# Sliding-window attention with soft expert mixing: logits a period later and ahead of the scores, the flip of x between two parts of the values, slot steps behind the second maxima

## The chip, the core and the metric

One core of a Trainium2 chip runs the whole program in one launch. The metric is the device time of that launch in microseconds (us); smaller is better. The time before is the median of three executions: 292.3 us (291.13 to 292.62).

## The reference

```python
scores = (q @ k.T) / 8                        # per batch and head, 8 x 8 of 576 x 64
scores = where(0 <= i - j < 128, scores - slope[head] * |i - j|, -1e9)
attn   = exp(scores - rowmax) / (rowsum + 1e-9)
x      = (attn @ v) as (8*576 tokens, 512)
logits = x @ phi                              # 512 x 32: 8 experts of 4 slots
d      = softmax of logits over all 4608 tokens
slot_input = d.T @ x                          # 32 x 512
slot_out[e] = relu(slot_input[e] @ w1[e]) @ w2[e]     # w1: 512 x 1024, w2: 1024 x 512
out    = (softmax of logits over the 32 slots) @ slot_out
```

Each query sees itself and the 127 keys before it. The softmax over all tokens needs every logit, so the expert layers can only begin once the attention of all tiles is done; the sums for the slots are kept as running maxima and running sums meanwhile.

## The kernel before

The program has two parts: a loop over 36 attention tiles, and a tail in which the weights w1 and w2 meet the 32 slot inputs and the output is written. A tile is 128 query rows (64 queries of each of two groups) with all 8 heads. Tile number t of a batch (t = 0 to 4) says which keys it sees; tile t = 0 sees no keys before its own, so its score products are narrower and its values have no second part.

Five engines work in their own order, which the order of the Python calls sets by hand (a manual schedule; nothing reorders the calls of one engine). The loop `for k in range(n)` (L589 to L632) is a software pipeline; one turn is called a period here. In period k the engines do, for different tiles:

- TensorE: `flip` (L299, products at L303) transposes the exponentials of tile k-1, group 0 into PSUM bank a, group 1 into bank b. `x_flip` (L361, products at L365) transposes the finished attention rows of tile k-3 into bank a again, so it has to wait until the copy of group 0 has left that bank. `values` (L325) multiplies by v for tile k-2, into banks e and o, in two parts: 32 products against whole blocks (L335; the PE queue records each of the 16 listed products in two passes), then 32 against half blocks (L345), which close the sums. Tile t = 0 has only the first part. Then `scores` for tile k+1, group 0 and group 1: the slope ramp (L233) and q times k (L246). They overwrite the score banks that the exponentials of tile k have read.
- ScalarE: `take` copies both groups of transposed exponentials out of PSUM (L306), `expo` computes the exponentials of tile k (L284, four per group), `x_keep` copies the transposed x (L368).
- GpSimd: `split` masks the copies in eight half-tile steps (L319, L322) and clears one column of a weight tile (L146), which gates the weight's load.
- VectorE: `chain` for each group of tile k, which is `merge` (L260), `rowmax` (L267) and `bias` (L272); then `x_store` of tile k-2 (L356 to L359), which divides by the row sums and frees banks e and o.
- SyncE issues all loads: q two tiles ahead, k a batch ahead, v four tiles ahead, and 35 of the weight units spread over the periods.

Every fourth tile closes a group q of four tiles for the expert part. Its steps are put into the periods by `do(when, k, ...)` (L567 to L580) and run by `run(when, k)` at named places of the loop: `logits` (L370, products at L375, into bank b) after the scores of period 4q+6, `token_copy` on ScalarE (L381) and `token_max` on VectorE (L386 to L390) after it, `token_exp` on ScalarE (L397); a period later `token_flips` (L416) and `slot_sum` (L428), both in bank b, `token_keep` (L422), `slot_add` (L438), and then the slot softmax on VectorE in small steps (`slots_max`, L450 and L451; `slots_norm`, L460 to L463), which are put into a list of fillers. At most four fillers were run at the end of each period, which is ahead of the next period's `chain`.

The buffers that matter: finished x rows have six places (`xns`, tile number modulo 6), transposed x four (`xts`, tile number modulo 4), and the PSUM banks a, b, e and o have one buffer each.

Of the kernel before, what the change touches and what calls it, by code (L numbers as in the profile page):

```python
# [25 lines left out]
NPAIR = H // 2  # L26
# [6 lines left out]
NQ = NTT // 4  # L33
# [32 lines left out]
def tile_attn_softmoe(  # L66
# [82 lines left out]
    st = {}  # L149
    last = B - 1  # L150

    def order(b):
        return (1, 2, 3, 4, 0) if b == last else range(4 + b % 2)

    tiles = [(b, t) for b in range(B) for t in order(b)]
# [103 lines left out]
    def merge(k, g, us=ALL):  # L259
        nc.vector.copy_predicated(  # L260
            window(k, g, us, 0, KB), bc(mask_le, 1, len(range(4)[us])), window(k, g, us, P, KB))
# [28 lines left out]
    def filler():  # L290
        if fillers:
            fillers.pop(0)()

    def chain(k, g):
        merge(k, g)
        rowmax(k, g)
        bias(k, g)
# [27 lines left out]
    def values(k, to=None):  # L325
        b, t = tiles[k]
        x = st["x", k] = to or [bank(tag, [P, NPAIR, VD], "xp") for tag in ("e", "o")]
        for j in range(NPAIR):
            for par in range(2):
                for g in range(2):  # L330
                    if t == 4:
                        v = (v3_even, v_slot[b, 3])[g]
                    else:
                        v = v_slot[b, t - 1 + g if t else 0]
                    nc.tensor.matmul(  # L335
                        x[par][half[g], j], lhsT=pas[k % 2][:, g, par, j], rhs=v[:, par, j],
                        start=(j == 0), stop=(t == 0 and j == NPAIR - 1))
        if t == 0:
            return
        for j in range(NPAIR):  # L340
            for par in range(2):
                for g in range(2):
                    rows = half[corner(k, g, par)]
                    v = (v4_even, v4_odd)[g] if t == 4 else v_slot[b, t - g]
                    nc.tensor.matmul(  # L345
                        x[par][half[g], j], lhsT=pps[k % 2][rows, g, j], rhs=v[rows, par, j],
                        start=False, stop=(j == NPAIR - 1))
# [121 lines left out]
    def drain():  # L469
        while fillers:  # L470
            filler()
# [57 lines left out]
    def do(when, k, fn, *a):  # L529
        todo.setdefault((when, k), []).append((fn, a))  # L530

    def run(when, k):
        for fn, a in todo.pop((when, k), []):
            fn(*a)
# [30 lines left out]
            load_v_tails(b + 1)  # L565

    for q in range(NQ - 1):  # L567
        k = 4 * q + 3
        do("post", k + 3, logits, q)
        do("act", k + 3, token_copy, q)  # L570
        do("dve", k + 3, token_max, q)
        do("late", k + 3, token_exp, q)
        do("dve", k + 4, token_sum, q)
        do("turn2", k + 4, token_flips, q)
        do("keep", k + 4, token_keep, q)
        do("mid", k + 4, slot_sum, q, "b")
        do("dve", k + 4, slot_add, q)
        do("dve", k + 4, later, slots_max, q)
        do("act", k + 5, slots_exp, q)
        do("dve", k + 5, later, slots_norm, q)  # L580
    for k in range(n - 3):
        do("turn", k + 3, x_flip, k)
        do("x_keep", k + 3, x_keep, k)
# [1 line left out]
    with tc.manual_schedule(engines=ORDERED):  # L585
# [3 lines left out]
        for k in range(n):  # L589
            if k:  # L590
                chain(k, 0)
            else:
                for us in (LO, HI):
                    merge(k, 0, us)
                    rowmax(k, 0, us)
                    bias(k, 0, us)
                    expo(k, 0, us)
            chain(k, 1)
            if k:
                flip(k - 1, 0, "a")  # L600
                flip(k - 1, 1, "b")
                run("turn", k)
                run("turn2", k)
            if k:
                take(k - 1, 0, nc.scalar.copy)
                split(k - 1, 0)
                load_weights_at(k, 1)
                take(k - 1, 1, nc.scalar.copy)
                split(k - 1, 1)
                load_weights_at(k, 2)  # L610
                expo(k, 0)
            run("keep", k)
            expo(k, 1)
            run("x_keep", k)
            if k >= 2:
                values(k - 2)
                after_values(k - 2)
            run("mid", k)
            if k + 1 < n:
                scores(k + 1, 0)  # L620
                scores(k + 1, 1)
                loads(k + 1)
            if k == n - 2:
                load_weight()
            run("post", k)
            if k >= 2:
                x_store(k - 2)
            run("act", k)
            run("dve", k)
            run("late", k)  # L630
            for _ in range(4):
                filler()  # L632

        ka, kb, kc = n - 3, n - 2, n - 1
        lp = free[3]
# [15 lines left out]
        x_flip(ka)  # L651
        x_keep(ka)
        values(kb)
        for _ in range(5):
            load_weight()
        values(kc, [x.rearrange("p (j d) -> p j d", d=P)[:, :, 0:VD] for x in (free[0], free[2])])
        x_store(kb)
        run("act", n)
        run("dve", n)
        x_store(kc, (0,))  # L660
# [277 lines left out]
```

## Time and profile before

| | |
|---|---|
| median of 3 executions | 292.3 us |
| the profiled execution's own time | 293.59 us |
| span of its records, first to last instruction | 291.9 us |
| time outside the span (293.59 - 291.9) | 1.69 us |
| TensorE matmuls busy | 253.2 us (87%) |
| VectorE busy | 178.9 us (61%) |
| ScalarE busy | 158.2 us (54%) |
| GpSimd busy | 97.6 us (33%) |
| mean granted TensorE clock | 0.994 |

The attention loop fills the span to about 222 us, the rest is the tail. In timelines a row gives start, time, engine, line, operation, operands and count, and in square brackets how long the engine stood idle before it and what ended that. PE is TensorE's products, PEld its weight loads, DVE VectorE, ACT ScalarE, POOL GpSimd. A weight load runs ahead of its product, so TensorE's pace from group to group is read from the starts of the PEld rows.

### The profile page before, as it was taken

What the parts mean: (1) busy time and instruction counts of PE and PEld (TensorE: products, weight loads), DVE (VectorE), ACT (ScalarE), POOL (GpSimd) and SP (SyncE); (2) the same over time, 40 slices, a digit from 0 to 9 for tenths busy, and PEclk for the clock granted to TensorE, in tenths of its full rate; (3) what the DMA queues carried; (4) which work ended last, traced back from release to release, by engine and by line L of the source; (5) the groups of instructions that cost most, each with busy time, mean ns of one, the idle gap of its engine ahead of it and who ended that gap; (6) DMA issues with size and microseconds to landing.
All of it is one profiled execution on the core that took longest, in us unless ns stands there. A gap on an engine that the chain in (4) does not pass through costs nothing.

```text
span 291.9 us, 12240 instructions
## 1 busy us (share of the span) xinstructions
PE 253.2 (87%) x5088; PEld 183.5 (63%) x5088; DVE 178.9 (61%) x550; ACT 158.2 (54%) x481; POOL 97.6 (33%) x269
## 2 busy tenths in 40 slices
PE   7688898988989897898899989989979889999980
PEld 3466776776777586666667757767766532566640
DVE  3566566775794875589478577657865741224461
ACT  2567756666755776656667566866565201013350
POOL 0046344541660566045417541645544001000000
PEclk9999999999999999999999999999999999999997
DMA  6769975788688477668776858855755999998895
GB/s 177 233 223 273 387 255 170 257 248 269 197 288 285 143 252 236 213 199 268 266 246 189 277 178 260 261 186 154 246 168 183 307 395 305 409 372 308 342 384 234
DMA packets 30715, 74.74 MB, mean 256 GB/s; under 512 B 3650, under 2 KB 5698, under 8 KB 30660
## 3 DMA queue, kind: packets, MB, share of 16 engines
q1 hardware_dynamic: 29940, 73.48, 75.5%
q8 instruction: 40, 0.66, 0.9%
q10 hardware_dynamic: 720, 0.48, 0.6%
q14 instruction: 15, 0.12, 0.1%
HBM read 64.51 MB, written 9.44 MB: 253 GB/s over the span
## 4 chain that ended last, share of the span: by engine, by line
PE 64%; DVE 14%; ACT 14%; issue 4%; DMA 1%; ACTq 0%; DVEq 0%
PE s L246 11%; PE xp L335 10%; PE xq L365 6%; ACT area L306 6%; PE op L772 5%; PE xp L345 5%; ACT area L284 5%; PE hp L736 5%; PE pt L303 5%; PE s L233 4%; PE po L793 4%; DVE nb L267 3%; PE lp L375 3%; PE ap L428 3%; DVE s L260 2%
## 5 line engine op out<-in xcount | busy, mean ns | idle before, releaser
L284 ACT ACTIVATE area<-s,nb 128x128 f32<-128x128 f32 x288 | 81.3, 393 | 9.5 <-DVE nb L272 8.2
L322 POOL TENSOR_SCALAR_AFFINE_SELECT area<-area 64x256 f32<-64x256 f32 x112 | 46.4, 414 | 116.1 <-ACT area L306 110.5
L306 ACT COPY area<-pt 128x512 f32<-128x512 f32 x71 | 38.0, 585 | 46.8 <-PE pt L303 46.0
L246 PE MATMUL s<-kq 64*64 64x192 f32 (+2 forms) x1088 | 53.7, 314 | 0.8 <-DMA kq<-k_t 0.8
L267 DVE TENSOR_REDUCE nb<-s 128x4 f32<-128x512 f32 (+1 forms) x73 | 49.9, 684 | 2.6
L319 POOL TENSOR_SCALAR_AFFINE_SELECT area<-area 64x256 f32<-64x256 f32 x112 | 46.1, 412 | 7.5
L246 PEld LDWEIGHTS s<-kq 64*64 64x64 f32 x1088 | 40.2, 138 | 3.8 <-DMA kq<-k_t 1.4
L335 PE MATMUL xp<-va,area 128*64 128x66 f32 x1120 | 40.9, 225 | 1.1 <-issue 1.1
L335 PEld LDWEIGHTS xp<-va,area 128*64 128x64 f32 x1120 | 35.7, 137 | 7.2 <-issue 4.0
L303 PE MATMUL pt<-unit_r,area 128*128 128x128 f32 x288 | 39.7, 280 | 0.6 <-DVE acc L438 0.6
L365 PE MATMUL xq<-unit_r,xs 128*128 128x128 f32 x144 | 23.7, 286 | 18.1 <-ACT area L306 17.0
L303 PEld LDWEIGHTS pt<-unit_r,area 128*128 128x128 f32 x288 | 30.7, 141 | 10.8 <-issue 7.9
L260 DVE COPY_PREDICATED s<-cst,s 128x256 f32<-128x256 int32 (+1 forms) x73 | 30.7, 420 | 9.1 <-PE s L246 8.9
L356 DVE TENSOR_SCALAR rs<-xp 128x4 f32<-128x4 f32 x70 | 8.7, 161 | 39.8 <-PE xp L345 36.4
L233 PE MATMUL s<-ramp 64*64 64x384 bf16 x288 | 26.5, 342 | 6.5 <-ACT area L284 5.6
L365 PEld LDWEIGHTS xq<-unit_r,xs 128*128 128x128 f32 x144 | 15.3, 141 | 26.2 <-ACT area L306 24.8
L359 DVE TENSOR_TENSOR xs<-xp,rs 128x256 f32<-128x256 f32 x70 | 26.5, 420 | 1.2
L368 ACT COPY xs<-xq 128x512 f32<-128x512 f32 (+1 forms) x36 | 22.7, 631 | 1.1 <-PE xq L365 1.0
L233 PEld LDWEIGHTS <-ramp 64*64 64x64 bf16 x288 | 11.6, 107 | 17.3 <-issue 15.8
L799 DVE COPY ob<-po 128x384 f32<-128x384 f32 x24 | 12.3, 553 | 13.1 <-PE po L793 12.5
L345 PE MATMUL xp<-va,area 64*64 64x66 f32 x896 | 19.6, 224 | 0.0
L799 ACT COPY ob<-po 128x384 f32<-128x384 f32 x24 | 10.3, 482 | 13.6 <-PE po L793 13.6
(112 smaller groups left out, 254.5 us busy)
## 6 DMA issues: line engine op xcount, KB each, us to landing
w<-w SPq DMA_DIRECT2D x49, 512.0 KB, 5.5
va<-v_n SPq DMA_DIRECT2D x36, 264.0 KB, 4.8
out<-ob SPq DMA_DIRECT2D x24, 384.0 KB, 4.1
kq<-q_t SPq DMA_DIRECT2D x35, 256.0 KB, 3.8
kq<-k_t SPq DMA_DIRECT2D x32, 256.0 KB, 4.3
xs<-w SPq DMA_DIRECT2D x5, 512.0 KB, 6.5
area<-w SPq DMA_DIRECT2D x4, 512.0 KB, 8.2
kt<-k_t SPq DMA_DIRECT2D x4, 384.0 KB, 5.2
```

Of the source, the lines that this page charges most:

```text
L233: nc.tensor.matmul(parts[par][half[c], :, 0:WIN], lhsT=slope[rows, c], rhs=steps[rows, 0 if t else 1 + g], start=True, stop=False)
L246: nc.tensor.matmul(parts[par][half[c], jh, KB * o:WIN], lhsT=qt[rows, j], rhs=keys, start=False, stop=(jh == 1))
L260: nc.vector.copy_predicated(window(k, g, us, 0, KB), bc(mask_le, 1, len(range(4)[us])), window(k, g, us, P, KB))
L267: nc.vector.tensor_reduce(s["nb"][:, 4 + us.start:4 + us.stop], window(k, g, us, 0, P), axis=AX.X, op=ALU.max, negate=True)
L284: nc.scalar.activation(dst, window(k, g, u, 0, P).rearrange("p (a w) -> p a w", a=2), AF.Exp, bias=s["nb"][:, u:u + 1], scale=SCALE)
L303: nc.tensor.transpose(s["pt"][:, u], s["p4"][:, u], ident)
L306: copy(pas[k % 2][:, g].rearrange("p a j m -> p (a j m)"), st[k, g]["pt"].rearrange("p u w -> p (u w)"))
L319: nc.gpsimd.affine_select(dst, pa, [[0, NPAIR], [-1, KB]], ALU.is_gt, 0.0, base=0, channel_multiplier=1)
L322: nc.gpsimd.affine_select(dst, pa, [[0, NPAIR], [1, KB]], ALU.is_ge, 0.0, base=0, channel_multiplier=-1)
L335: nc.tensor.matmul(x[par][half[g], j], lhsT=pas[k % 2][:, g, par, j], rhs=v[:, par, j], start=(j == 0), stop=(t == 0 and j == NPAIR - 1))
L345: nc.tensor.matmul(x[par][half[g], j], lhsT=pps[k % 2][rows, g, j], rhs=v[rows, par, j], start=False, stop=(j == NPAIR - 1))
L365: nc.tensor.transpose(st["xq", k][:, P * j:P * j + P], xns[k % NXN][:, P * j:P * j + P], ident)
```

## The change

The second part of the values becomes a function of its own (`values_ex`, L339, products at L347), and the calls of a period are put in another order. Numbers of the lines behind it rise by 2 in the functions (`x_flip` at L367, logits at L377, slot sums at L430).

```diff
-        if t == 0:
-            return
-        for j in range(NPAIR):
+
+    def values_ex(k):
+        b, t = tiles[k]
+        x = st["x", k]
+        for j in range(NPAIR if t else 0):
...
     for q in range(NQ - 1):
-        k = 4 * q + 3
-        do("post", k + 3, logits, q)
-        do("act", k + 3, token_copy, q)
-        do("dve", k + 3, token_max, q)
-        do("late", k + 3, token_exp, q)
-        do("dve", k + 4, token_sum, q)
-        do("turn2", k + 4, token_flips, q)
-        do("keep", k + 4, token_keep, q)
-        do("mid", k + 4, slot_sum, q, "b")
-        do("dve", k + 4, slot_add, q)
-        do("dve", k + 4, later, slots_max, q)
-        do("act", k + 5, slots_exp, q)
-        do("dve", k + 5, later, slots_norm, q)
+        k = 4 * q + 6 + (q < NQ - 2)
+        do("mid" if q < NQ - 2 else "post", k, logits, q)
+        do("act", k, token_copy, q)
+        do("dve", k, token_max, q)
+        do("late", k, token_exp, q)
+        do("dve", k + 1, token_sum, q)
+        do("turn2", k + 1, token_flips, q)
+        do("keep", k + 1, token_keep, q)
+        do("mid", k + 1, slot_sum, q, "b")
+        do("dve", k + 1, slot_add, q)
+        do("dve", k + 1, later, slots_max, q)
+        do("act", k + 2, slots_exp, q)
+        do("dve", k + 2, later, slots_norm, q)
...
             chain(k, 1)
+            for _ in range(4):
+                filler()
             if k:
                 flip(k - 1, 0, "a")
                 flip(k - 1, 1, "b")
-                run("turn", k)
-                run("turn2", k)
+            if k >= 2:
+                values(k - 2)
+            run("turn", k)
+            run("turn2", k)
...
             expo(k, 1)
-            run("x_keep", k)
             if k >= 2:
-                values(k - 2)
+                values_ex(k - 2)
                 after_values(k - 2)
             run("mid", k)
+            run("x_keep", k)
...
             run("late", k)
-            for _ in range(4):
-                filler()
...
         values(kb)
+        values_ex(kb)
...
         x_store(kb)
+        drain()
         run("act", n)
```

On TensorE the order inside every period changes. This is a period of the second batch, around one `x_flip`; xp is written by the values, xq by `x_flip`, s by the scores, pt by `flip`:

```order
 L246 MATMUL s_1_87<-kq 64x128 x8
 L303 MATMUL pt<-unit_r,area 128x128 x8
-L365 MATMUL xq<-unit_r,xs 128x128 x4
-L335 MATMUL xp<-va,area 64x66 x16
-L345 MATMUL xp<-va,area 64x66 x16
+L335 MATMUL xp<-va,area 64x66 x16
+L367 MATMUL xq<-unit_r,xs 128x128 x4
+L347 MATMUL xp<-va,area 64x66 x16
 L233 LDWEIGHTS ramp
 L233 MATMUL s_0_86<-ramp 64x2x192
```

The first part of the values now stands between the transposes of the exponentials and those of x, and the second part behind the latter.

On TensorE around the logits of the first group (lp), before: they stand behind the scores, and the next period has the flips of the logits (dp) and the slot sums (ap).

```order
L246 MATMUL s_1_87<-kq 64x192 x8
L375 MATMUL lp<-xs,phi 32x128 x16
L303 MATMUL pt<-unit_r,area 128x128 x8
L365 MATMUL xq<-unit_r,xs 128x128 x4
L416 MATMUL dp<-unit_r,lg 128x128 x2
L335 MATMUL xp<-va,area 64x66 x16
L345 MATMUL xp<-va,area 64x66 x16
L428 MATMUL ap<-xs,dn 32x512 x4
```

The same logits in the changed kernel, one period later:

```order
L303 MATMUL pt<-unit_r,area 128x128 x8
L335 MATMUL xp<-va,area 64x66 x16
L367 MATMUL xq<-unit_r,xs 128x128 x4
L347 MATMUL xp<-va,area 64x66 x16
L377 MATMUL lp<-xs,phi 32x128 x16
L233 LDWEIGHTS ramp
L233 MATMUL s_0_86<-ramp 64x2x192
```

They now stand ahead of that period's scores. For the last group but one (q = 7) they stay in period 34 behind the scores.

On VectorE, behind the first slot steps, before: the four steps of `slots_norm` (cs, ln) stand between `x_store` (xs) and the next maxima (nb).

```order
L359 TENSOR_TENSOR xs<-xp,rs 128x256 x2
L460 TENSOR_REDUCE cs<-ln 128x4
L461 TENSOR_SCALAR cs<-cs 128x4
L462 RECIPROCAL cs<-cs 128x4
L463 TENSOR_TENSOR ln<-ln,cs 128x128
L260 COPY_PREDICATED s_0_86<-cst,s_0_86 128x4x64
L267 TENSOR_REDUCE nb<-s_0_86 128x4
```

The same steps in the changed kernel:

```order
L260 COPY_PREDICATED s_1_87<-cst,s_1_87 128x4x64
L267 TENSOR_REDUCE nb<-s_1_87 128x4
L272 TENSOR_SCALAR nb<-nb 128x4
L462 TENSOR_REDUCE cs<-ln 128x4
L463 TENSOR_SCALAR cs<-cs 128x4
L464 RECIPROCAL cs<-cs 128x4
L465 TENSOR_TENSOR ln<-ln,cs 128x128
L358 TENSOR_SCALAR rs<-xp 128x4 x2
```

They stand behind both groups' maxima and ahead of the next `x_store`. The order of ScalarE and of GpSimd inside a period stays; the group steps alone come one period later there. Because the slot sums of group q are now read in period 4q+8, and `x_store` of that same period writes tile 4q+6 into the place of tile 4q, that `x_store` has to wait for the slot sums.

## The prediction

> **What bounds the kernel now.** I read the page first, then the waits summed by pair, then the rows of single periods.
>
> ```profile
> PE 253.2 (87%) x5088; PEld 183.5 (63%) x5088; DVE 178.9 (61%) x550; ACT 158.2 (54%) x481; POOL 97.6 (33%) x269
> ```
>
> Of the span of 291.9 us TensorE works 87% and the next engine 61%, so what TensorE waits for in the loop is what can be won. The summed waits name it (total us, times, longest):
>
> ```profile
> PEld xq L365 <- ACT area L306: 24.8, 33, 1.5
> ...
> ACT lg L381 <- PE lp L375: 16.3, 8, 3.4
> ...
> ACT area L284 <- DVE nb L272: 8.2, 12, 3.2
> ...
> PE s L233 <- ACT area L284: 5.6, 10, 1.8
> ```
>
> The flip of x waits in every period for ScalarE's copy out of bank a, 24.8 us in all. The two next rows delay ScalarE: it stands for the logits, and for late maxima. The last is TensorE waiting to overwrite scores that are still being read. Now one period without group steps on TensorE, by its weight loads:
>
> ```profile
> 199.68 0.86 PEld L303 LDWEIGHTS pt<-unit_r,area 128*128 128x128 f32 x8 [0.28 <-issue]
> 201.06 0.42 PEld L365 LDWEIGHTS xq<-unit_r,xs 128*128 128x128 f32 x4 [0.53 <-ACT area L306]
> 201.65 1.01 PEld L335 LDWEIGHTS xp<-va,area 128*64 128x64 f32 x32 [0.17 <-POOL area L322]
> 202.73 0.56 PEld L345 LDWEIGHTS xp<-va,area 64*64 64x64 f32 x32
> 203.20 0.12 PEld L233 LDWEIGHTS <-ramp 64*64 64x64 bf16 x4
> 203.26 0.64 PEld L246 LDWEIGHTS s<-kq 64*64 64x64 f32 x16
> 203.91 0.13 PEld L233 LDWEIGHTS <-ramp 64*64 64x64 bf16 x4
> 204.07 0.64 PEld L246 LDWEIGHTS s<-kq 64*64 64x64 f32 x16
> 204.99 0.31 PEld L303 LDWEIGHTS pt<-unit_r,area 128*128 128x128 f32 x3 [0.28 <-issue]
> ```
>
> The next flips start at 204.99, so the period is 204.99 - 199.68 = 5.31 us. Of that 0.53 us is the wait for the copy; the work is 4.78 us. The same stretch on ScalarE, VectorE and GpSimd:
>
> ```profile
> 200.43 1.07 ACT L306 COPY area<-pt 128x512 f32<-128x512 f32 x2 [2.80 <-PE pt L303]
> 201.39 2.19 ACT L284 ACTIVATE area<-s,nb 128x128 f32<-128x128 f32 x8
> ```
> ```profile
> 203.47 0.25 DVE L356 TENSOR_SCALAR rs<-xp 128x4 f32<-128x4 f32 x2 [1.31 <-PE xp L345]
> 203.75 0.20 DVE L357 RECIPROCAL rs<-rs 128x8 f32<-128x8 f32 x1
> 203.99 0.76 DVE L359 TENSOR_TENSOR xs<-xp,rs 128x256 f32<-128x256 f32 x2
> 204.66 0.28 DVE L460 TENSOR_REDUCE cs<-ln 128x4 f32<-128x128 f32 x1
> ...
> 205.60 0.42 DVE L260 COPY_PREDICATED s<-cst,s 128x256 f32<-128x256 int32 x1
> ```
> ```profile
> 204.61 0.41 POOL L322 TENSOR_SCALAR_AFFINE_SELECT area<-area 64x256 f32<-64x256 f32 x1
> ```
>
> VectorE does the slot steps from 204.66 to 205.60, 0.94 us, while the next scores already wait for their maxima. In periods where this is later still, the exponentials are late, and TensorE with them.
>
> **The first part of the values ahead of the flip of x.** Counted from the start T of a period's flips: the first copy starts at T + 0.75 (200.43) and lets the flip of x go at T + 1.38 (201.06). In the new order 0.86 us of flips, a gap of 0.17 and 1.08 us of values come first, so the flip of x can start at T + 2.11, when the copy is 0.7 us old. The 24.8 us go. What is ready for the values? Their copies and masks are a period old: GpSimd's last mask ends at 204.61 + 0.41 = 205.02, T + 5.34, and the next values start at the next T + 0.86, which is T + 5.86 if a period is 5.0: 0.5 us to spare. Banks e and o are freed at 203.99 + 0.76 = 204.75, T + 5.1: 0.8 us to spare. Lateness beyond that would be paid in full in each period. SyncE's issues keep their places; the loads of v wait for the second part as before.
>
> The order costs changes of operand shape. Now there are flips to x flips, x flips to values (0.17 gap), and values part to part (0.07). After: flips to values, values to x flips, x flips to second part. Gaps at changes lie between none and 0.28 us in the rows above, so the extra is between 0 and 2 x 0.28 - 0.17 = 0.39; I take 0.2, one gap like that ahead of L335. TensorE's period becomes 4.78 + 0.2 = 4.98.
>
> **What is late next: ScalarE.** The exponentials end at 201.39 + 2.19 = 203.58, T + 3.90, and scores of group 1 may not start before. How a period looks that is held by that:
>
> ```profile
> 59.35 2.40 ACT L284 ACTIVATE area<-s,nb 128x128 f32<-128x128 f32 x8 [1.07 <-DVE nb L272]
> 61.79 0.36 PE L233 MATMUL s<-ramp 64*64 64x384 bf16 x4 [0.25 <-ACT area L284]
> 62.73 0.86 PEld L303 LDWEIGHTS pt<-unit_r,area 128*128 128x128 f32 x8 [0.28 <-issue]
> ```
>
> The scores go 0.04 us after the exponentials, and the next flips 0.94 us later. So ScalarE allows a period of 3.90 + 0.04 + 0.94 = 4.88. That this ring turns at such a pace is seen at the start, in a period with no x to flip:
>
> ```profile
> 16.82 1.09 PE L303 MATMUL pt<-unit_r,area 128*128 128x128 f32 x8
> ```
> ```profile
> 21.71 1.09 PE L303 MATMUL pt<-unit_r,area 128*128 128x128 f32 x8
> ```
>
> 21.71 - 16.82 = 4.89 us. The two limits, 4.98 and 4.88, lie close; a quiet period is 5.0 us. Without second part it is held at 4.89; with narrow scores it gains a third of the 0.64 us load of group 1 and is 4.67 (an estimate from 128 columns in place of 192).
>
> **Slot steps behind the second maxima.** This takes up to 0.94 us from the path of `x_store` to the maxima. VectorE then does the steps while it would wait for the values (1.31 us idle before 203.47), so they cost nothing; without that idle time 0.94 us once in four periods, 7 us in all. The maxima of group 1 have to be there at T + 2.8, when ScalarE has done half of its 2.19 us.
>
> **Logits ahead of the scores, a period later.** One group's rows:
>
> ```profile
> 190.96 0.81 PEld L375 LDWEIGHTS lp<-xs,phi 128*32 128x32 f32 x32 [0.28 <-issue]
> 191.97 0.88 PEld L303 LDWEIGHTS pt<-unit_r,area 128*128 128x128 f32 x8 [0.20 <-issue]
> 192.11 0.27 ACT L381 COPY lg<-lp 128x128 f32<-128x128 f32 x1 [2.08 <-PE lp L375]
> ```
> ```profile
> 194.37 0.42 PEld L365 LDWEIGHTS xq<-unit_r,xs 128*128 128x128 f32 x4 [1.52 <-ACT area L306]
> ```
> ```profile
> 195.71 0.40 ACT L422 COPY dn<-dp 128x256 f32<-128x256 f32 x1
> ```
> ```profile
> 197.93 0.11 PEld L233 LDWEIGHTS <-ramp 64*64 64x64 bf16 x4 [0.84 <-issue]
> ```
>
> The copy of the logits came only with the next flips, ScalarE stood 2.08 us for it, its copies of the flips were late, and TensorE stood 1.52 us. In the new order the logits are done one pair of scores (1.79 us, 203.20 to 204.99) earlier, under ScalarE's own `x_keep`; the copy, maximum and exponential then end just as the next flips are ready. That `x_keep` now waits for the logits, whose place it overwrites; they end about 0.4 us after the exponentials, off the path. The logits themselves stay 1.01 us of TensorE, plus 0.1 for changed gaps: 6.1 us for such a period. The period behind it lasted from 191.97 to 199.68, 7.71 us; less 1.52 it is 6.19, plus 0.2 for the shapes and 0.1 because the slot sums now come so early that they wait for the 0.40 us copy of the flipped logits: 6.5. A new wait is that of `x_store` for the slot sums in that period. Behind it on VectorE stand the running sums and the next maxima; the sums end about 1.0 us after the values do, and the maxima of group 0 are needed at the next T + 1.7 (201.39), so I take zero (bounds 0 and 1.0 us, seven times).
>
> **The sum.** Flips in the rows of the loop:
>
> ```profile
> 26.33 1.09 PE L303 MATMUL pt<-unit_r,area 128*128 128x128 f32 x8
> ```
> ```profile
> 210.50 1.09 PE L303 MATMUL pt<-unit_r,area 128*128 128x128 f32 x8
> ```
> ```profile
> 222.15 0.66 PE L303 MATMUL pt<-unit_r,area 128*128 128x128 f32 x4
> ```
>
> From period 4 to the end of period 35 the loop takes 222.15 - 26.33 = 195.8 us. After: 16 quiet periods (11 at 5.0, 2 at 4.89, 3 at 4.67) 78.8; 7 with logits (5 at 6.1, 2 without second part, 0.47 and a gap of 0.15 less, at 5.48) 41.5; 7 with slot sums (3 at 6.5, 2 narrow, two thirds of group 0's 0.64 and a third of group 1's less, at 5.86, 2 without second part, held by the copy, at 6.35) 43.9; the last two, where the logits stay behind the scores, 11.6 as before (222.15 - 210.50). Together 175.8, a gain of 20.0 us. I take two things off. TensorE also stood without a wait that the trace names:
>
> ```profile
> 29.44 1.04 PE L335 MATMUL xp<-va,area 128*64 128x66 f32 x28 [0.80 <-issue]
> ```
> ```profile
> 114.04 0.33 PE L365 MATMUL xq<-unit_r,xs 128*128 128x128 f32 x1 [1.11 <-issue]
> ```
> ```profile
> 21.70:38.50 16.80, 14.91 (x352) 12.34 (x348) 10.76 (x33) 11.09 (x33) 7.30 (x21) 1.00 0.98 325
> 38.50:222.20 183.70, 163.64 (x3589) 127.68 (x3585) 130.16 (x409) 120.65 (x376) 85.17 (x230) 1.00 0.72 226
> ```
>
> These stalls, 1.9 us, I leave in. And up to 38.5 us the DMA engines are busy 0.98 of the time (last but one column) with 325 GB/s: there the loads cannot come 2 us earlier. I take 1.0 off (bounds 0 and 2.2). In the rest of the loop the share is 0.72 and would be about 0.80. The tail keeps its work; its two slot steps now stand ahead of the last `x_store` (0.6 us late), while the last slot sums come up to 0.7 earlier: zero.
>
> 20.0 - 1.9 - 1.0 = 17.1 us. The profiled execution, 293.59 us (span 291.9 and 1.69 outside), would be 276.5; it lay 1.3 above the median, so the median would be 292.3 - 17.1 = 275.2, called 275.
>
> **The rivals.**
> *The wait moves to the maxima.* VectorE is busy 130.16 us of 183.70 in the loop, 71%, and would be 79% of 165. If `x_store` and the maxima slip, the exponentials wait again, as in the 8.2 us row. A loss of 0.25 us in 28 periods is 7 us: 282. For it: that row; against it: 1.31 us of idle time before `x_store`.
> *Shape changes cost a whole product.* The upper bound of 0.39, plus as much around logits and slot sums, 30 times 0.3: 9 us, 284. The Trainium skill, "TensorE: Matmul & The Clock Gate", Part 3 (Packing small matmuls), says that weight loads overlap running products only when their row groups differ; full-height flips between values would then each wait out a product. The trace bears it out in part only: the eight full-height loads of L303 take 0.86 us, 0.11 each, one behind the other. By that rule the sum would be this rival's 284.
> *Loads.* With a DMA share of 0.98 up to 38.5 us, 2.2 us are lost instead of 1.0, and about five more stalls of 1 us come: 281.
> *Nothing.* The whole wait comes back as a wait of the scores for the exponentials, with a period of 5.31 as now: 292. Against it stands the period of 4.89.
> *Slower.* Each of the two new shape changes costs what stands ahead of 197.93, 0.84 us: 32 x (1.68 - 0.2) = 47 us, 322. It turns to slower from 0.2 + 17.1/32 = 0.73 us for both together. That row stands behind the slot sums, with 512 columns a product, which speaks against it.
>
> **How the numbers follow.** Forecast (270 to 280) 0.60; maxima 0.14; shapes 0.08; loads 0.09; nothing 0.05; slower 0.04. The low end: with no shape cost (0.2 x 24 + 0.1 x 7 = 5.5 us) and the 1.9 and 1.0 us won as well the time is 267. The high end takes in the first three rivals: 285. The runs before spread over 0.5% (291.13 to 292.62), about what can be told from no change. Faster 0.91, same 0.05, slower 0.04.
>
> **What would show it.** Right: the wait of the x flips for the copies nearly gone, quiet periods of 4.9 to 5.1 us, short waits of scores for exponentials (up to 0.3 us each), ScalarE's wait for the logits under 3 us in all. Wrong: quiet periods of 5.2 or more, a large row of the second part or the x flips with idle time ahead, or exponentials waiting for maxima as before.

## The result, and the profile after

The changed kernel takes 276.76 us (median of 4 executions, 273.5 to 278.58); the kernel before took 292.46 us beside it (291.13 to 293.06). The ratio is 0.940, with a 95% interval of 0.931 to 0.949. Here and in the table further down the ratios leave out executions more than 1.5% above the fastest of their kernel, here two of the four (277.69 and 278.58 us); the quotient of the two medians is 0.946. The forecast was 275 us, 267 to 285.

The profiled execution of the changed kernel took 273.5 us, with a span of 271.8 us. Busy time of the engines, from its page:

```profile
PE 249.7 (92%) x5088; PEld 182.8 (67%) x5088; DVE 178.4 (66%) x550; ACT 158.9 (58%) x481; POOL 97.4 (36%) x269
```

The busy times are nearly those of before; the span became shorter, and TensorE's share rose from 87% to 92%. What went is idle time. The summed waits of the changed kernel (total us, times, longest) name it:

```profile
DVE xs L361 <- PE ap L430: 6.2, 7, 1.9
...
PE s L233 <- ACT area L284: 4.9, 8, 1.8
...
PEld ap L430 <- ACT dn L424: 1.8, 3, 0.7
...
ACT lg L383 <- PE lp L377: 1.4, 1, 1.4
...
PEld xq L367 <- ACT area L306: 0.9, 2, 0.5
...
ACT area L284 <- DVE nb L272: 0.8, 3, 0.3
```

The wait of the flip of x for the copy fell from 24.8 to 0.9 us, ScalarE's wait for the logits from 16.3 to 1.4 us (only the last group but one, which stays in its old place), and that of the exponentials for late maxima from 8.2 to 0.8 us. New is the first row: `x_store` waits for the slot sums, as the change makes it.

The 24.8 us of before are idle time of the weight loads, which run ahead. The products' own row for the same wait was smaller, because earlier products still ran in part of that time:

```profile
PE xq L365 <- ACT area L306: 17.0, 33, 1.3
```

In the changed kernel that row is 0.5 us.

A quiet period of the changed kernel, by TensorE's weight loads:

```profile
168.09 0.86 PEld L303 LDWEIGHTS pt<-unit_r,area 128*128 128x128 f32 x8 [0.28 <-ACT ln L457]
169.12 1.01 PEld L335 LDWEIGHTS xp<-va,area 128*64 128x64 f32 x32 [0.17 <-issue]
170.20 0.42 PEld L367 LDWEIGHTS xq<-unit_r,xs 128*128 128x128 f32 x4
170.79 0.56 PEld L347 LDWEIGHTS xp<-va,area 64*64 64x64 f32 x32 [0.17 <-issue]
171.25 0.13 PEld L233 LDWEIGHTS <-ramp 64*64 64x64 bf16 x4
171.31 0.64 PEld L246 LDWEIGHTS s<-kq 64*64 64x64 f32 x16
171.96 0.15 PEld L233 LDWEIGHTS <-ramp 64*64 64x64 bf16 x4
172.12 0.64 PEld L246 LDWEIGHTS s<-kq 64*64 64x64 f32 x16
173.04 0.20 PEld L303 LDWEIGHTS pt<-unit_r,area 128*128 128x128 f32 x2 [0.28 <-issue]
```

From flips to flips it is 173.04 - 168.09 = 4.95 us, against 5.31 before: the wait of 0.53 us is gone and 0.17 us of gaps are new. The flip of x stands at 170.20 without a wait in brackets. The gaps at changes of operand shape are 0.17 us ahead of the first part, 0.07 ahead of the flip of x (169.12 + 1.01 to 170.20) and 0.17 ahead of the second part: 0.17 us more than before. ScalarE in the same period:

```profile
168.79 1.07 ACT L306 COPY area<-pt 128x512 f32<-128x512 f32 x2 [0.99 <-PE pt L303]
169.75 2.19 ACT L284 ACTIVATE area<-s,nb 128x128 f32<-128x128 f32 x8
```
```profile
172.12 0.34 PE L233 MATMUL s<-ramp 64*64 64x384 bf16 x4
```

The exponentials end at 169.75 + 2.19 = 171.94 us, and the first products of group 1's scores, which must not come before that, start at 172.12 without a wait. TensorE's own work and ScalarE's ring (its copies and exponentials, then TensorE's scores behind them) are now 0.2 us apart or less at this point.

The loop, from the flips of period 4 to those of period 36:

```profile
25.17 1.09 PE L303 MATMUL pt<-unit_r,area 128*128 128x128 f32 x8
```
```profile
201.99 1.09 PE L303 MATMUL pt<-unit_r,area 128*128 128x128 f32 x8 [0.46 <-ACT xs L370]
```

It takes 176.8 us instead of 195.8: 19.0 us. The tail behind it is unchanged (291.9 - 222.15 = 69.75 before, 271.8 - 201.99 = 69.81 after). The other 1.2 us of the span's 20.1 are an earlier start of the loop (25.17 against 26.33). The medians differ by 15.7 us, since the profiled execution lay 1.1 us above its median before and 3.3 us below it after.

### The profile page after: what moved, and what is told of

It reads as the page before. It is cut to its first block, busy times and chain, and to the rows that moved or that the text cites. A ratio compares the mean times of both kernels' runs of the same rounds, so it can differ in the third digit from the quotient of the medians.

```text
span 271.8 us, 12284 instructions
## 1 busy us (share of the span) xinstructions
PE 249.7 (92%) x5088; PEld 182.8 (67%) x5088; DVE 178.4 (66%) x550; ACT 158.9 (58%) x481; POOL 97.4 (36%) x269
## 4 chain that ended last, share of the span: by engine, by line
PE 73%; ACT 10%; DVE 9%; issue 3%; DMA 3%; ACTq 0%; DVEq 0%
PE s L246 13%; PE pt L303 10%; PE xp L335 10%; ACT area L284 6%; PE op L778 6%; PE xq L367 6%; PE hp L742 5%; PE s L233 5%; PE xp L347 5%; PE po L799 4%; PE lp L377 3%; PE ap L430 3%; ACT area L306 3%; DMA kq<-k_t 3%; DVE nb L267 2%
## 5 line engine op out<-in xcount | busy, mean ns | idle before, releaser
L306 ACT COPY area<-pt 128x512 f32<-128x512 f32 x71 | 38.2, 588 | 41.8 <-PE pt L303 41.7
L246 PE MATMUL s<-kq 64*64 64x192 f32 (+2 forms) x1088 | 51.9, 306 | 1.5 <-DMA kq<-k_t 1.4
L246 PEld LDWEIGHTS s<-kq 64*64 64x64 f32 x1088 | 39.1, 134 | 4.4 <-DMA kq<-k_t 1.7
L370 ACT COPY xs<-xq 128x512 f32<-128x512 f32 (+1 forms) x36 | 22.1, 614 | 3.2 <-PE lp L377 2.4
L367 PE MATMUL xq<-unit_r,xs 128*128 128x128 f32 x144 | 23.5, 286 | 0.5 <-ACT area L306 0.5
L347 PE MATMUL xp<-va,area 64*64 64x66 f32 x896 | 19.6, 224 | 0.0
L347 PEld LDWEIGHTS xp<-va,area 64*64 64x64 f32 x896 | 15.7, 133 | 4.6 <-issue 4.5
```

The costliest lines, as they stand in the source:

```text
L246: nc.tensor.matmul(parts[par][half[c], jh, KB * o:WIN], lhsT=qt[rows, j], rhs=keys, start=False, stop=(jh == 1))
L306: copy(pas[k % 2][:, g].rearrange("p a j m -> p (a j m)"), st[k, g]["pt"].rearrange("p u w -> p (u w)"))
L347: nc.tensor.matmul(x[par][half[g], j], lhsT=pps[k % 2][rows, g, j], rhs=v[rows, par, j], start=False, stop=(j == NPAIR - 1))
L367: nc.tensor.transpose(st["xq", k][:, P * j:P * j + P], xns[k % NXN][:, P * j:P * j + P], ident)
```

## The experiments

My theory: the three parts of the change remove three different delays (the copy that the flip of x waits for; the logits that ScalarE waits for; the late maxima), each at another place of the loop, so their gains add up. The rivals: they are one slack seen three times, so that one part alone brings most of it; or a part brings nothing. Every kernel ran beside the kernel before on its own chip. The loop's time, split by kinds of period, is worked out from the starts of the flips of periods 4 to 36 in the traces; the parts are rounded, so they can miss the sum by 0.1. Five kernels have their logits one period earlier than the changed one (before, values split alone, slot steps alone, all but the logits, and logits ahead, not later). Their columns hold other tiles: the seven periods with slot sums have no narrow scores there and two with narrow scores in the changed kernel. Between the two kinds of kernel only the column of all periods compares directly:

```
us of the loop           7 with   7 with     last   16        all     median of runs,
                         logits   slot sums  two    others            ratio to before [95%]
before                   44.5     52.4       11.7   87.4     195.8
changed                  41.9     42.9       11.4   80.6     176.8    276.76  0.940 [0.931, 0.949]
values split alone       42.5     48.2       11.4   84.9     187.0    283.58  0.974 [0.968, 0.979]
logits alone             44.5     45.9       12.3   88.9     191.6    288.17  0.986 [0.977, 0.995]
slot steps alone         43.6     52.3       11.7   82.0     189.5    289.32  0.994 [0.989, 0.998]
all but the split        43.8     45.4       11.7   83.9     184.8    282.16  0.968 [0.962, 0.973]
all but the logits       43.0     48.2       11.4   78.6     181.2    279.5   0.961 [0.954, 0.968]
all but the slot steps   41.3     42.5       12.0   87.5     183.4    282.05  0.968 [0.963, 0.974]
second part ahead too    41.5     46.4       11.4   80.5     179.8    278.9   0.949 [0.940, 0.957]
logits behind scores     41.7     47.0       11.4   80.2     180.3    279.14  0.959 [0.952, 0.967]
logits ahead, not later  50.5     43.8       11.4   79.2     184.9    284.05  0.966 [0.959, 0.973]
no second part           38.2     42.1       11.4   79.4     171.0    269.67  0.917 [0.911, 0.923]
seven places for x       44.5     43.1       11.4   79.7     178.6    275.76  0.935 [0.928, 0.943]
seven, loads later       43.2     42.7       11.4   78.9     176.2    275.62  0.943 [0.936, 0.950]
```

### Each part alone, and each part taken back

The split of the values in the kernel before, with its old table for the logits and the slot steps at the period's end:

```diff
-                run("turn", k)
-                run("turn2", k)
+            if k >= 2:
+                values(k - 2)
+            run("turn", k)
+            run("turn2", k)
...
             if k >= 2:
-                values(k - 2)
+                values_ex(k - 2)
```

> Only the first part of the values goes ahead of the flip of x; logits and slot steps stay where they were. Theory (three delays, each with its own cure): TensorE's wait for the copy out of bank a goes, about 25 us to under 5, but two quiet periods in four still have 0.57 or 0.94 us of slot steps ahead of the maxima and stay near 5.5 us, about 7 us over the loop, and the late logits cost 2 more: 281 to 284 us. Rival (the flip of x is the whole gain): 276 to 278 us. Rival (the wait only moves to the maxima): 287 us or more.

The changed kernel with the split taken back, so that both parts stand behind the flip of x again:

```diff
-            if k >= 2:
-                values(k - 2)
-            run("turn", k)
-            run("turn2", k)
+            if k:
+                run("turn", k)
+                run("turn2", k)
...
             if k >= 2:
+                values(k - 2)
                 values_ex(k - 2)
```

> The changed kernel with all values behind the flip of x again. Theory: TensorE waits 0.53 us for the copy out of bank a in each period, about 17 us in all, and saves 0.2 us of shape changes in each; periods without second part or with narrow scores are held by ScalarE anyway, so it costs 5 to 9 us: 281 to 285 us. Rival (shape changes eat the gain): 277 us. Rival (the flip of x is the whole gain): 289 us or more.

The logits: the new table and the new place of `x_keep` alone, and the changed kernel with the old ones (this is the second's edit; the table's other rows are left out here):

```diff
-        k = 4 * q + 6 + (q < NQ - 2)
-        do("mid" if q < NQ - 2 else "post", k, logits, q)
+        k = 4 * q + 3
+        do("post", k + 3, logits, q)
...
+            run("x_keep", k)
             if k >= 2:
                 values_ex(k - 2)
                 after_values(k - 2)
             run("mid", k)
-            run("x_keep", k)
```

> Only the logits move (a period later, ahead of the scores); values and slot steps as before the change. Theory: TensorE's wait of 1.52 us behind the logits falls to the usual 0.53, 1.0 us in each of 7 groups: 284 to 287 us. Rival (ScalarE's wait for the logits was off the path): 291 to 293 us.

> The changed kernel with the logits back in their old place and period; split and slot steps as changed. Theory: ScalarE stands about 2 us for the logits again in each of 7 groups, but the first part of the values covers most of its late copies, and TensorE loses some 0.3 to 0.5 us a group: 278 to 280 us. Rival (the logits' move carries a large part, 1 us of TensorE a group and the late maxima behind it): 283 us or more.

The slot steps: behind `chain(k, 1)` alone, and the changed kernel with them at the period's end (again the second's edit):

```diff
             chain(k, 1)
-            for _ in range(4):
-                filler()
...
             run("late", k)
+            for _ in range(4):
+                filler()
...
         x_store(kb)
-        drain()
```

> Only the slot steps move behind the second maxima. Theory: most of the 8.2 us that exponentials waited for maxima, and half of the 5.6 us that scores waited for exponentials, go, but TensorE's wait for the copy stays: 286 to 289 us. Rival (no effect while the copy holds TensorE): 291 to 293 us.

> The changed kernel with the slot steps back between the storing of x and the first maxima. Theory: in two periods of four the maxima of group 1 are 0.3 to 0.6 us late for ScalarE and the period is held by that, 5.2 to 5.5 us in place of 4.95: 280 to 283 us, with waits of exponentials for maxima of 4 to 8 us in all. Rival (VectorE has room enough): 277 us, no such waits.

Measured: four of the six medians lie in their ranges; logits alone (288.17) and slot steps alone (289.32) lie 1.2 and 0.3 us above theirs. At a threshold of 2%, slot steps alone count as no change, and logits alone stay undecided.

In the loop the parts alone take off 8.8, 4.2 and 6.3 us, together 19.3; taken back out of the whole they cost 8.0, 4.4 and 6.6 us, together 19.0. The whole is 19.0. That these agree so closely is partly luck, since each trace holds from none to three stalls of TensorE that have no named cause (last section), 1.9 us of them in the kernel before. If those of 0.3 us or more are taken off at full length, an estimate, the parts alone are 8.2, 4.3 and 4.4 us, together 16.9, those taken back 7.6, 3.2 and 7.1, together 18.0, and the whole is 17.9. So the gains add up within about 1 us, and the slot steps are worth more beside the other parts (7.1) than alone (4.4). The rival of one slack falls: no part alone brings most of the whole, and each is missed when it is taken back.

The times agree with this but can't show it as finely. By the ratios of the table the parts alone bring 2.6, 1.4 and 0.6%, together 4.7%, the whole 6.0%, and taking a part back costs 2.8, 2.1 and 2.8%, together 7.7%; each has an uncertainty of 0.5 to 1%. For the slot steps alone the medians show 2.3 us where the loop shows 6.3. Of the 6.3 us, 1.9 are the two stalls of the kernel before (the prediction's rows at 29.44 and 114.04), which this trace doesn't have; and its span is only 4.2 us shorter (287.7 against 291.9), since its loop starts 1.3 us later and its tail is 0.8 us longer.

Slot steps alone shorten above all the other periods (87.4 to 82.0). Logits alone shorten the periods with slot sums, in full size from 7.71 (7.34 in the first group) to between 6.65 and 6.70 us; the column's 52.4 to 45.9 is more, because two of its periods now have narrow scores. The split shortens all kinds by some. The waits show why a part isn't enough. Of the split alone:

```profile
ACT lg L383 <- PE lp L377: 13.7, 8, 2.2
ACT area L284 <- DVE nb L272: 8.1, 10, 3.1
...
PEld xq L367 <- ACT area L306: 2.9, 8, 0.5
```

The wait of the flip of x falls from 24.8 to 2.9 us, but the loop only by 8.8: what is late next are the two rows that the other parts remove, almost as large as before (16.3 and 8.2). Of the changed kernel without the split:

```profile
PEld xq L367 <- ACT area L306: 18.0, 33, 1.5
PE xq L367 <- ACT area L306: 10.2, 33, 1.3
```

The wait is back in all 33 periods, yet it costs 8.0 us, not 17. In a quiet period 0.17 us of its 0.53 are spent anyway, in the split's gaps, so 0.36 us remain (5.31 against 4.95); and periods with narrow scores or without a second part are alike in both kernels (4.68, 4.62 and 4.89 us), which fits ScalarE's ring as their limit. The products' row, 10.2 us, is nearer to the cost than that of the weight loads. Of the changed kernel with the slot steps at the period's end:

```profile
PE s L233 <- ACT area L284: 9.3, 21, 1.7
ACT area L284 <- DVE nb L272: 9.1, 16, 3.0
```

Maxima are late 16 times (3 times in the changed kernel), exponentials behind them, and scores behind those 21 times instead of 8. The full-size periods with slot steps take 5.5 to 5.8 us there.

### Ahead of the scores, or only later

The logits of the changed kernel behind the scores of the same period (later, not ahead); and ahead of the scores in the old period (ahead, not later):

```diff
-        do("mid" if q < NQ - 2 else "post", k, logits, q)
+        do("post", k, logits, q)
```

> The changed kernel with the logits a period later but behind the scores, as before the change. Theory: ScalarE stands for the logits again, since they come with the next flips; same cost as taking the logits' whole move back: 278 to 281 us. Rival (the later period is what counts, because the transposed x is ready): 276 to 277 us.

```diff
-        k = 4 * q + 6 + (q < NQ - 2)
+        k = 4 * q + 6
...
+            run("x_keep", k)
             if k >= 2:
                 values_ex(k - 2)
                 after_values(k - 2)
             run("mid", k)
-            run("x_keep", k)
```

> The changed kernel with the logits ahead of the scores but in the old period, in which ScalarE copies the last of the four transposed x. Theory (the later period is needed): TensorE waits for that copy, which ScalarE does only behind all exponentials, about 4.7 us into the period, while TensorE is there at 3.4: 1 to 1.5 us in each of 7 groups, 283 to 288 us. Rival: the copy is in time, 277 us.

Later alone:

```profile
ACT lg L383 <- PE lp L377: 13.4, 8, 1.8
```

ScalarE waits 13.4 us for the logits as if nothing had been moved (1.4 in the changed kernel), and the periods with slot sums take 47.0 us in place of 42.9. So most of the gain, 3.5 of 4.4 us of the loop, is from the place ahead of the scores. Ahead alone doesn't do either:

```profile
PEld lp L377 <- ACT xs L370: 6.6, 7, 1.1
```

In the old period the logits need the x that `x_keep` copies in that same period, and TensorE's weight loads stand in front of them 0.94 us in each of seven periods (6.6 / 7). A full-size period with logits takes 7.1 to 7.3 us there, in place of 6.1. The later period takes this wait away; the earlier place brings most of the gain. Both times (279.14 and 284.05 us) lie in their ranges.

### The second part of the values

Both parts ahead of the flip of x:

```diff
             if k >= 2:
                 values(k - 2)
+                values_ex(k - 2)
             run("turn", k)
             run("turn2", k)
...
-                values_ex(k - 2)
```

> The changed kernel with both parts of the values ahead of the flip of x, so the order is flips, first part, second part, flip of x, scores. The covers are the same; only the order of shapes differs. Theory (a change of shape costs a gap of up to 0.28 us): the flip of x behind 64-row loads has a gap of about 0.28, and 0.17 behind it, in place of 0.07 and 0.17 and none: 0.1 to 0.4 us more in a quiet period, 278 to 284 us. Rival (gaps come from waits, not shapes): 276 to 277 us.

The changed kernel without the products of the half blocks; it leaves that part of the attention out:

```diff
-                        start=(j == 0), stop=(t == 0 and j == NPAIR - 1))
+                        start=(j == 0), stop=(j == NPAIR - 1))
...
-        for j in range(NPAIR if t else 0):
+        for j in range(0):
```

> The changed kernel without the second part of the values: the products of the half blocks are left out, all else is done. This takes 0.59 us of TensorE (and a gap) from each quiet period and nothing from ScalarE. Theory (ScalarE's ring is the next limit, 4.88 us): quiet periods fall only from 4.95 to 4.85 to 4.90, and the time by 2 to 6 us, mostly in periods with logits; scores wait 0.3 to 0.5 us for exponentials in each period. Rival (TensorE alone holds the loop): quiet periods of 4.4 us, 15 us less.

Both parts ahead, the middle of a quiet period:

```profile
172.11 1.01 PEld L335 LDWEIGHTS xp<-va,area 128*64 128x64 f32 x32 [0.17 <-issue]
173.20 0.56 PEld L347 LDWEIGHTS xp<-va,area 64*64 64x64 f32 x32
173.83 0.42 PEld L367 LDWEIGHTS xq<-unit_r,xs 128*128 128x128 f32 x4
174.42 0.11 PEld L233 LDWEIGHTS <-ramp 64*64 64x64 bf16 x4 [0.17 <-issue]
```

From the first part to the ramp it is 174.42 - 172.11 = 2.31 us, in the changed kernel 171.25 - 169.12 = 2.13; the whole quiet period is 5.07 us, 0.12 longer. This order of shapes costs a tenth of a microsecond, no more; the gap of 0.28 us expected ahead of the flip of x measures 0.07 (173.20 + 0.56 to 173.83). The loop is 2.9 us longer. The periods with slot sums take 3.5 us more (46.4 against 42.9), 1.4 of them in one period that also holds an unnamed stall of 0.53 us. In these periods the slot sums now wait for the later flipped logits:

```profile
PEld ap L430 <- ACT dn L424: 5.7, 8, 0.8
```

That wait is 5.7 us in place of 1.8. The median, 278.9 us, lies in the range, but two of the four executions took 276.5 and 276.8 us, as the rival has it, and the ratio's interval overlaps that of the changed kernel: the time decides nothing here, the rows do.

Without the second part TensorE has 0.46 us less to do in a period (170.79 to 171.25 above). A quiet period of this kernel, by the products:

```profile
183.34 1.09 PE L303 MATMUL pt<-unit_r,area 128*128 128x128 f32 x8
...
187.29 0.36 PE L233 MATMUL s<-ramp 64*64 64x384 bf16 x4
...
188.23 0.55 PE L303 MATMUL pt<-unit_r,area 128*128 128x128 f32 x3
```
```profile
185.05 2.19 ACT L284 ACTIVATE area<-s,nb 128x128 f32<-128x128 f32 x8
```

In all, scores wait there more often for exponentials than in the changed kernel (4.9 us, 8 times):

```profile
PE s L233 <- ACT area L284: 8.3, 19, 1.7
```

The quiet period lasts 188.23 - 183.34 = 4.89 us, where TensorE's work would allow about 4.5. Group 1's scores start at 187.29, 0.05 us behind the end of the exponentials at 187.24: this is ScalarE's ring of 4.88, now the bound. In the quiet periods of the changed kernel the two limits lie 0.07 us apart; the 7.1 us by which this kernel is faster (269.67 against 276.76; 5.8 in the loop) are more than the 2 to 6 expected and come for the greater part from the periods with logits (38.2 against 41.9).

### The wait of x_store, and the first loads

Finished x rows get seven places instead of six, so that `x_store` no longer writes into the place that the slot sums read. Room for it comes from laying the table of the mask and slopes (`cst`) and the last factors (`comb`) into parts of other buffers that are free at that time, and the places of some weight units among the x rows shift with it:

```diff
-NXN = 6
+NXN = 7
...
-    cst = cpool.tile([P, CW], F32, name="cst")
+    cst = lg[:, HW - CW:]
...
-    comb = cpool.tile([P, NS], F32, name="comb")
+    comb = kt[:, 0:NS]
```

> The changed kernel with seven places for finished x rows in place of six, so that the storing of x does not wait for the slot sums in the period after the logits (the mask constants and a small tile move into spare columns to make room). Theory: the 6 us that VectorE waits there is mostly covered, but the maxima behind it are late in the period that follows, which lasts 5.5 us in two groups: 0.5 to 2 us less than the changed kernel, 275 to 276 us. Rival: covered in full, no difference. Rival: it holds every group, 4 us less or more.

The same, and the loads of weight units begin in period 5 instead of 2:

```diff
-W0 = 2
+W0 = 5
```

> Seven places for finished x rows as above, and the loads of weights for the tail begin in period 5 in place of period 2. Theory (loads crowd the first periods, DMA share near 1): periods 4 to 6, 5.0 to 5.5 us before, come down to about 4.95, 1 us in all, and the share later in the loop rises a little without holding it: 273 to 275 us. Rival (stalls of the first periods do not come from the weights): no difference to seven places alone, 275 to 277 us.

First the changed kernel in periods 8 and 9, on VectorE, ScalarE and TensorE:

```profile
51.83 0.76 DVE L361 TENSOR_TENSOR xs<-xp,rs 128x256 f32<-128x256 f32 x2 [0.49 <-PE ap L430]
52.50 0.14 DVE L412 COPY fine<-sb 128x1 f32<-128x1 f32 x1
52.56 0.68 DVE L443 COPY acc<-ap 128x512 f32<-128x512 f32 x1
```
```profile
56.23 1.14 ACT L284 ACTIVATE area<-s,nb 128x128 f32<-128x128 f32 x4 [0.30 <-DVE nb L272]
```
```profile
57.43 0.36 PE L233 MATMUL s<-ramp 64*64 64x384 bf16 x4 [0.36 <-ACT area L284]
```

`x_store` stands 0.49 us for the slot sums, the running sums stand behind it, and all that follows on VectorE is later: the exponentials of group 1 wait 0.30 us for their maxima and the scores 0.36 us for the exponentials. Period 9 takes 5.51 us, period 13 likewise 5.50. With seven places period 9 is:

```profile
55.73 0.86 PEld L303 LDWEIGHTS pt<-unit_r,area 128*128 128x128 f32 x8 [0.17 <-issue]
...
60.67 0.20 PEld L303 LDWEIGHTS pt<-unit_r,area 128*128 128x128 f32 x2 [0.28 <-issue]
```

60.67 - 55.73 = 4.94 us, and period 13 takes 5.02 (4.95 and 5.14 with the loads later too). So the new wait costs 0.57 + 0.48 = 1.05 us, in two periods of seven; the five others behind slot sums are alike in both kernels (4.68, 4.62, 4.94, 4.89, 4.94 and 4.67, 4.63, 4.95, 4.88, 4.95). These two follow the only slot-sum periods with narrow scores, which take 5.65 us where the others take 6.2 to 6.6; that the maxima are therefore needed too early is argued, not shown. The kernel's time can't show a gain this small: 275.76 us lies in the expected range, but the interval overlaps that of the changed kernel, and the profiled execution, at 278.74 us, has a stall of its own (below).

With the loads later, the start of the loop is as the theory has it:

```profile
21.00:37.00 16.00, 15.89 (x374) 13.31 (x365) 11.95 (x35) 11.06 (x34) 7.33 (x20) 1.00 0.72 225
```

The DMA share there (last but one column) is 0.72; in the changed kernel it was 0.97. Periods 4 to 6 take 5.03, 4.95 and 4.89 us instead of 5.29, 5.21 and 5.45: 1.1 us less, half of it in period 6, where the changed kernel has an unnamed stall (the row at 38.52 below). Other kernels that load as early as the changed one, with a DMA share of 0.97 and 0.95, have 15.1 us (second part ahead too) and 15.4 us (seven places) for these three periods, against 15.95 in the changed kernel and 14.87 here, so how much of it is the loads stays open. The time, 275.62 us, lies above the expected range and in that of the rival, and isn't measurably below that of the changed kernel. No version that I ran beats it beyond the uncertainty.

## Why the prediction was right, point by point

- *The first part of the values ahead of the flip of x.* Right: the wait went from 24.8 to 0.9 us, and taking this part back costs 8.0 us of loop. The flip of x starts 2.11 us behind the period's flips (170.20 - 168.09), as worked out. It was right not to book the 24.8 us as a gain, but to add up periods with their new limits: the split alone brought 8.8.
- *Changes of operand shape, taken as 0.2 us a period (0 to 0.39).* Measured 0.17. The rival with a product's wait for each change falls: the full-height load of the flip of x begins 0.07 us behind the last load of the first part, and at 170.20 us ahead of the end of that part's last product (169.12 + 1.15 = 170.27 by the products' row). The rule that the prediction takes from the Trainium skill, "TensorE: Matmul & The Clock Gate", Part 3 (Packing small matmuls), by which this order would have come out at 284 us, isn't borne out here.
- *Quiet period 5.0 us, from 4.98 on TensorE and 4.88 on ScalarE.* Measured 4.95, and 4.89 where TensorE has less to do: both limits were right. Narrow ones were put at 4.67, and measured 4.62 to 4.68.
- *Logits: 41.5 us for seven periods.* Measured 41.9. That the copy of the logits then comes in time is seen in the changed kernel:

```profile
176.36 0.81 PEld L377 LDWEIGHTS lp<-xs,phi 128*32 128x32 f32 x32
177.37 0.11 PEld L233 LDWEIGHTS <-ramp 64*64 64x64 bf16 x4 [0.20 <-issue]
```
```profile
177.46 0.59 ACT L370 COPY xs<-xq 128x512 f32<-128x512 f32 x1 [0.52 <-PE lp L377]
177.94 0.27 ACT L383 COPY lg<-lp 128x128 f32<-128x128 f32 x1
```

  `x_keep` waits 0.52 us for the logits, the copy of the logits follows without a wait, and the logits cost TensorE 177.37 - 176.36 = 1.01 us, as in the sum.
- *Slot sums: 43.9 us for seven periods.* Measured 42.9. A full-size period was put at 6.5 us, with 0.1 for the slot sums' wait for the flipped logits, and the three measured 6.28 (narrow ones 5.65 for 5.86, those without second part 6.19 and 6.56 for 6.35):

```profile
181.46 0.42 PEld L367 LDWEIGHTS xq<-unit_r,xs 128*128 128x128 f32 x4
181.84 0.25 PEld L418 LDWEIGHTS dp<-unit_r,lg 128*128 128x128 f32 x2
182.26 0.56 PEld L347 LDWEIGHTS xp<-va,area 64*64 64x64 f32 x32 [0.17 <-issue]
182.89 0.16 PEld L430 LDWEIGHTS ap<-xs,dn 128*32 128x32 f32 x8
```

  The second part of the values stands between the flips of the logits and the slot sums, and these start 0.07 us behind it without a wait.
- *The new wait of `x_store`, taken as zero (0 to 1.0 us, seven times).* Mis-sized: 1.05 us in two of seven periods. The prediction had the running sums and the next maxima in its count and still took the slack as enough for all seven; in the first two groups it wasn't.
- *Sixteen other periods, 78.8 us.* Measured 80.6: 1.0 us of it is `x_store`'s wait, and 1.06 us are periods 4 to 6 (15.95 against 5.0 + 5.0 + 4.89), of which period 6 with the stall below is 0.56. The prediction had 1.0 us for crowded loads; that they are the cause isn't shown.
- *Unnamed stalls, 1.9 us left in.* In this profile 0.79 us:

```profile
38.52 0.34 PE L335 MATMUL xp<-va,area 128*64 128x66 f32 x5 [0.79 <-issue]
```

- *The tail, zero.* Right within 0.1 us.
- *The sum.* The loop was put at 195.8 - 17.1 = 178.7 us and measured 176.8. The gain at the median, 15.7 us, is below the 17.1 forecast, that of the profiled execution, 20.1, above it. The profiled execution was put at 276.5 us and took 273.5, while the median lies 3.3 us above it where the prediction counted on 1.3 below. These two errors nearly cancel, so that 276.76 us lies so near to 275 is in part luck.

## What to carry to other kernels

When an engine waits at one place in each period, move the work that is ready ahead of the wait, but size the gain by the next limit (here ScalarE's ring and the late maxima) and by what the new order costs (0.17 us a period), not by the wait: 24.8 us of waiting were worth 8.8. Delays that end on different engines at different places of a software pipeline have to be removed each; here their gains added up within about 1 us. A step that is moved takes its buffer's lifetime along: reading x a period later put a wait on the writer of that buffer, and whether it costs is decided by what is queued behind that writer.

## What the runs showed of the hardware that was not expected

- TensorE stands now and then for 0.5 to 1.5 us where the trace names no releaser. No trace has more than three of them in the loop, and those of all but the slot steps, slot steps alone and no second part have none. In five kernels one lies at the same product of the first part in period 6, 38 to 41 us into the span (the row at 38.52 above); others lie elsewhere, as with seven places for x:

```profile
117.15 0.54 PE L246 MATMUL s<-kq 64*64 64x192 f32 x4 [1.31 <-issue]
```

  Their places are not random. Number TensorE's records, weight loads and products together, in the order of their starts. In the 14 traces 21 gaps between products of 0.3 us or more, in loop and tail, have no named releaser, and the count of records ahead of each leaves 192, 193 or 194 when divided by 256: 1217 for the row at 38.52, 4545 for that at 117.15, 706 and 4034 for the two stalls of the kernel before. A loop passes some 30 such places (24 without the second part) and stands 0.3 us or more at three of them at most. This speaks for something that comes round every 256 of TensorE's instructions, such as their supply, and not for the work at that place. What it is no run shows, and no experiment was made on it.
- Executions of one kernel lie up to 9.25 us apart (276.47 to 285.72 for the second part ahead too; 273.65 to 281.31 for seven places with later loads). The start of the loop alone moves from 25.15 to 28.64 us between the traces of the kernels. That start and the stalls would account for the difference between the gain at the median and that of the profile; that they do is argued, not shown.
- One execution of the kernel with the logits ahead in the old period took 474.11 us where its others took 282 to 285. Nothing that I have explains it.
